# Clustered attention followed by a SwiGLU layer on one core: how q and k of groups 3 to 7 are loaded and transposed

## The chip, the cores and the metric

The kernel runs on one core of a Trainium2 chip. The metric is device time in microseconds (us), the median of several runs. A profile of one execution is used beside it; its times are counted from the start of its span.

## The reference, cut to what matters

Attention in which a query only sees the keys of its own cluster, then a gated feed-forward layer over all heads:

```python
B, H, S, D = 4, 8, 768, 64            # 16 centroids for each head
q_assign = argmax(q_n @ c_n.T); k_assign = argmax(k_n @ c_n.T)    # nearest centroid
mask = q_assign[..., :, None] == k_assign[..., None, :]
scores = where(mask, q @ k.T / sqrt(D), -1e9)
attn = softmax(scores) @ v
x = attn.transpose(0, 2, 1, 3).reshape(B * S, H * D)              # 3072 x 512
xn = x / rms(x) * rms_g
out = (silu(xn @ w_gate) * (xn @ w_val)) @ w_out                  # 512 -> 1536 -> 512
```

All inputs and the output are float32 in HBM.

## The kernel before, in words

**Groups and units.** The 32 (batch, head) pairs are numbered n = 0 to 31 and taken in eight groups of four heads (g = 0 to 7, so a batch is two groups). The attention and the feed-forward work run in eight units of half a batch: unit u covers 384 queries of batch u // 2 for all eight heads. A unit has 24 gaps (8 heads, three each); at each gap `scores` (line 323) issues two score matmuls, L333, and one exponential on ScalarE, L337. `pv` (line 341) multiplies the probabilities with v, L351, and VectorE divides and stores, L356 and L358.

**The mask.** For each head a tile `qext` or `kext` holds the transposed q or k in 64 rows and a one-hot of its cluster in 16 further rows, so that one matmul of depth 80 gives the scores and the mask. Both have four buffers, one for each of four groups.

**From HBM to `qext` and `kext`.** `load` (line 80) brings q or k of one head to a staging tile `qk` with 128 partitions, in each six tokens of 64 numbers, 1536 bytes without a break. The tile holds q and k; there are six (`NQ`), so the load of head n + 6 waits until head n has been used. `trans` (line 202) transposes with three TensorE matmuls against an identity (L208) into a PSUM tile `tq`; ScalarE (L214), or VectorE for some heads of the second batch (L212), copies it to `qkT` and scales k by 1/2048 on the way. `cast` (line 220, instruction L227) makes bf16 halves of 64 partitions of it, on GpSimd for q, on VectorE for k in group 3 and later. `cluster_steps` (line 255) multiplies with the centroids (L241), transposes (L244), finds the largest and makes the one-hot (L249, L253), transposes back (L271), and `place` (line 277) sends it with 16 small DMAs (L282) to the last rows of `qext` and `kext`: 8 for q and 8 for k. For group 2 these 16 DMAs are issued by SyncE's queue (SP), for groups 3 to 7 by GpSimd's (POOL). Groups 0 and 1 are placed by VectorE (`under`, L317).

**What sets the order.** The order on each engine is written out. Unit 0 uses a table of work for each gap, `first`. In the other units `attention` (line 636) walks through the gaps and fills in work from a list, each piece with a cost; pieces are issued so that the summed cost keeps pace with the gaps. `group_work` (line 468), which makes the pieces of one group, gives each `trans` 0.3 and the rest of the preparation mostly 0. Unit 1 does the casts of group 2 and the transposes of group 3; unit u from 2 to 5 prepares group u + 2. The feed-forward work of earlier units makes up the rest: `gv` (gate and val, L423, with the tanh L431 and the products L432 and L436 on VectorE) and `out_mm` (L448). Gate, val, tq, sc, tx and o take turns in the three PSUM buffers of the tag `gen`.

**The SP queue.** It issues, in order, the loads of q, k and v, the 16 DMAs of `place` of group 2, and the stores of the output. In the stretch that matters it issues: q and k of heads 12 and 13, v of heads 8 to 15, q and k of head 14, v 16, q and k of 15, v 17, q and k of 16, v 18, q and k of 17, v 19, then `place` of group 2 (four DMAs for the first half of q, eight for k, four for the second half of q), then q, k and v of later heads. The load of v 16 waits until GpSimd has read v 8 (L230). The DMAs of the SP and ACT queues share eight semaphores in turn, and each DMA waits for the landing of the one eight before it. The weights are loaded by GpSimd's queue (L194, L197), with a cast to bf16, four pairs of w_gate and w_val and three pieces of w_out.

**Squares.** `squares` (L373 on VectorE, L376 on ScalarE) sums the squares of a unit's rows; VectorE does it for units 0 and 1, ScalarE for the rest.

Of the kernel before, what the change touches and what calls it, by code (L numbers as in the profile page):

```python
# [18 lines left out]
ZS = 2048.0  # L19
# [3 lines left out]
def kernel(  # L23
# [12 lines left out]
    nc = tc.nc  # L36
    B, H, S, D = q.shape
# [5 lines left out]
    HT = ST // 2  # L43
    UQ = HT * P
    HG = 4
# [8 lines left out]
    CUT = CC + 2 * FC - 8  # L54
    LEAD = 6
    NQ, NV = 6, 8

    ctx.enter_context(tc.manual_schedule())
    pool = lambda n, b, **kw: ctx.enter_context(tc.tile_pool(name=n, bufs=b, **kw))
# [14 lines left out]
    staged, stagedv = {}, {}  # L74

    def src(a, n):
        b, h = divmod(n, H)
        return a[b, h].rearrange("(p t) d -> p t d", t=ST)

    def load(n, part, on=None):  # L80
        if n not in staged:
            staged[n] = stage.tile([P, 2, ST, D], F32, tag="qk", name="qk")
        (on or nc.sync).dma_start(out=staged[n][:, part], in_=src((q, k)[part], n))

    def load_qk(n):
        if n < B * H:
            load(n, 0)
            load(n, 1)

    def load_v(n, vq=None):  # L90
        if n >= B * H:
            return
        stagedv[n] = stage.tile([P, ST, D], F32, tag="vs", name="vs", bufs=NV)
        (vq or nc.sync).dma_start(out=stagedv[n], in_=src(v, n))

    c_in = const.tile([P, D], F32)
    nc.sync.dma_start(out=c_in, in_=centroids.rearrange("h c d -> (h c) d"))
    load(0, 0)
    load(0, 1, nc.scalar)
    load(1, 1, nc.scalar)  # L100
# [49 lines left out]
    for i in range(P // 32):  # L150
        r = slice(32 * i, 32 * i + 32)
# [48 lines left out]
    qkT = {}  # L200

    def trans(g, h, part, on=None):
        if (g, h // 2) not in qkT:
            qkT[g, h // 2] = qk32.tile([P, 2, 2, UQ], F32, tag="qkT", name="qkT")
        qk = staged[g * HG + h]
        ps = ps_g.tile([P, UQ], F32, tag="gen", name="tq")
        for i in range(HT):
            nc.tensor.transpose(ps[:, i * P:(i + 1) * P], qk[:, part, 2 * i:2 * i + 2].rearrange("p t d -> p (t d)"),  # L208
                                ident_f)
        to, by = qkT[g, h // 2][:, h % 2, part], 1.0 / ZS if part else 1.0  # L210
        if on is nc.vector:
            nc.vector.tensor_scalar_mul(to, ps, by)  # L212
        else:
            nc.scalar.activation(to, ps, ACT.Copy, scale=by)  # L214

    def cols(of, g, e, a=0, b=UQ):

        return of.rearrange("p (x e) -> p x e", e=2)[:, a:b, e] if g < H // HG else of[:, e * UQ + a:e * UQ + b]

    def cast(on, g, h, part, es=(0, 1)):  # L220
        for e in es:
            to = cols((kext if part else qext)[g % 4][:D, h], g, e)
            of = qkT[g, h // 2][e * D:(e + 1) * D, h % 2, part]
            if on is nc.scalar:
                nc.scalar.copy(to, of)
            else:
                on.tensor_copy(to, of)  # L227

    def vcast(n):
        nc.gpsimd.tensor_copy(vbf[n // HG % 4][:, n % HG, :, :D], stagedv[n])  # L230
# [24 lines left out]
    def cluster_steps(g, m):  # L255

        of = {}

        def products():
            of["cl"] = cluster_products(g, [(h, m) for h in range(HG)])  # L260

        def most():
            of["mx"] = largest(of["cl"])

        def same():
            of["ohT"] = asg.tile([P, UQ], BF16, tag="ohT", name="ohT", bufs=2)
            compare(of["ohT"].rearrange("p (b e c) -> p b e c", e=2, c=NC), of["cl"], of["mx"])

        def back():
            put[g, m] = asg.tile([P, UQ], BF16, tag="oh", name="oh", bufs=3)  # L270
            nc.vector.transpose(put[g, m], of["ohT"])  # L271

        return [products, most, same, back]
# [3 lines left out]
    def place(on, g, m, es=(0, 1)):  # L277

        ext = (kext if m else qext)[g % 4]
        for h in range(HG):  # L280
            for e in es:
                on.dma_start(out=ext[D:D + NC, h, e * UQ:(e + 1) * UQ],  # L282
                             in_=put[g, m][32 * h + e * NC:32 * h + (e + 1) * NC])
# [82 lines left out]
    def squares(u, t, last):  # L366
        if (t, last) == (0, False):
            sq[u] = small.tile([P, 2, HT], F32, tag="ss", name="ss")
            xn[u] = xp.tile([P, HT, DM], BF16, tag="xn", name="xn")
        c = slice(DM - 2 * D, DM) if last else slice(0, DM - 2 * D)  # L370
        to = sq[u][:, int(last), t:t + 1]
        if u <= 1:
            nc.vector.scalar_tensor_tensor(xn[u][:, t, c], xs[u][:, t, c], 1.0 / DM, xs[u][:, t, c], op0=ALU.mult,  # L373
                                           op1=ALU.mult, accum_out=to)
        else:
            nc.scalar.activation(xn[u][:, t, c], xs[u][:, t, c], ACT.Square, scale=DM ** -0.5, accum_out=to)  # L376

    def rms(u):
        x, nt = xs[u], UNITS[u][2]
        for t in range(nt):  # L380
            squares(u, t, True)
        ms = small.tile([P, HT], F32, tag="ms", name="ms")
        nc.vector.scalar_tensor_tensor(ms[:, :nt], sq[u][:, 0, :nt], 1e-6, sq[u][:, 1, :nt], op0=ALU.add, op1=ALU.add)
        y = rsqrt(ms[:, :nt], nt)
        for t in range(nt):
            nc.vector.tensor_scalar_mul(xn[u][:, t], x[:, t], y[:, t:t + 1])
# [81 lines left out]
    def group_work(g):  # L468

        t, c = [], []  # L470
        for h in range(HG):
            n = g * HG + h
            t += [(0.3, lambda h=h: trans(g, h, 0)), (0.3, lambda h=h: trans(g, h, 1))]

            def others(n=n):
                vcast(n)
                load_qk(n + NQ)
                load_v(n + NV)

            def both(h=h, f=others):  # L480
                cast(nc.gpsimd, g, h, 0)
                f()
                cast(nc.vector, g, h, 1, (0,))
            if g == 2:
                c.append((0.0, others))
            else:
                c += [(0.0, both), (0.0, lambda h=h: cast(nc.vector, g, h, 1, (1,)))]
        a = []
        for m in range(2):
            a += [(0.0 if i else 0.7, f) for i, f in enumerate(cluster_steps(g, m))]  # L490
            if g == 3:
                a.append((0.0, lambda m=m: place(nc.gpsimd, g, m)))
            elif g == 2:
                a.append((0.0, (lambda: (place(nc.sync, g, 1), place(nc.sync, g, 0, (1,)))) if m else
                          (lambda: place(nc.sync, g, 0, (0,)))))
        if g > 3:
            a[:1] = [(1.4, lambda f=(a[0][1], a.pop(4)[1]): [x() for x in f])]
            a.append((0.0, lambda: [place(nc.gpsimd, g, m) for m in range(2)]))
        return t, c, a
# [5 lines left out]
    def group(g):  # L505
        t, c, a = group_work(g)
        return [x for h in range(HG) for x in t[2 * h:2 * h + 2] + c[2 * h:2 * h + 2]] + a
# [13 lines left out]
    def ffn_work(u):  # L521
        n = UNITS[u][2] / HT
        w = [(0.18 * n, lambda c=c: xtrans(u, c)) for c in range(CC)]
        for f in range(FC):
            for val in (False, True):
                w.append((0.64 * n, lambda f=f, val=val: gv(u, f, val)))
        return w

    def out_work(u):
        return [(0.86, lambda t=t, p=p: out_mm(u, t, p)) for t in range(UNITS[u][2]) for p in range(3)]  # L530
# [6 lines left out]
    def tokens(g, h, on=None):  # L537
        trans(g, h, 1, on)
        trans(g, h, 0, on)
# [96 lines left out]
    def attention(heads, fill, skip=0, hooks={}):  # L636
        gaps = [(u, h, i) for u, h in heads for i in range(UNITS[u][2])]
        total, done, n = sum(c for c, _ in fill), 0.0, 0
        for at, (u, h, i) in enumerate(gaps):
            scores(u, h, i)  # L640
            if i == (0 if (u, h) == (1, 0) else 1):
                for p in due:
                    pv(*p)
                due[:] = [(u, h)]
            if h == H - 1:
                squares(u, i, False)
            if (u, h, i) in hooks:
                hooks[u, h, i]()
            while n < len(fill) and at >= skip and done <= total * (at + 1 - skip) / (len(gaps) - skip):
                done += fill[n][0]  # L650
                fill[n][1]()
                n += 1
        for _, f in fill[n:]:
            f()

    attention([(0, h) for h in range(H)], [], hooks={(0, *divmod(i, HT)): f for i in range(H * HT) for f in [first.get(i, more)] if f})
    for u in range(1, NU):
        ffn, o, g = ffn_work(u - 1), out_work(u - 2) if u > 1 else [], u + 2
        if u == 1:
            t, c, a = group_work(2)  # L660
            t3, c3, a3 = group_work(3)
            n = LEAD - 4
# [60 lines left out]
```

The softmax here doesn't subtract the row's maximum and nothing guards it: scores larger than these inputs give would overflow.

## Time and profile before

| what | value |
|---|---|
| median of 3 runs | 345.44 us (345.31 to 345.99) |
| span of the profiled execution | 343.6 us |
| its own time | not recorded apart from the runs; they are 1.7 to 2.4 us above the span |
| TensorE busy | 336.0 us, 98% of the span |
| VectorE busy | 219.9 us, 64% |
| ScalarE busy | 259.7 us, 76% |
| GpSimd busy | 112.9 us, 33% |
| granted TensorE clock | 1.000 |
| transposes L208 | 192, of 276 ns each |
| first score matmul of units 1 to 5 | 33.1, 64.8, 106.6, 147.6, 188.7 us |

A row of the costliest groups reads: line, engine, operation, output<-inputs, shapes, count, then the busy time and the mean length of one, then the idle time of the engine just before them and what ended it. The timeline has start, length, engine, line and operation; neighbours of a kind are merged, and "x4" says how many. Matmuls overlap: the length of one says less than the distance from one start to the next. The answer on DMA gives, for a stretch, the packets and the share of the 16 DMA engines of each queue: q1 is the SP queue, q0 is GpSimd's. Below it are the DMAs issued in the stretch, with the median time from issue to landing.

### The profile page before, as it was taken

Reading aid. Unit: us, or ns where it says so; the run is one execution under the profiler, and the core shown is the slowest. Engines: PE = TensorE matmul, PEld = TensorE weight load, DVE = VectorE, ACT = ScalarE, POOL = GpSimd, SP = SyncE. Lnnn points to the kernel's source line nnn. Section 1 sums busy time; section 2 is a strip of 40 time slices with the busy share of each in tenths; the row PEclk is TensorE's granted clock in tenths of the full one; section 3 lists DMA queues with packets and bytes.
Section 4 is the critical chain, followed back from the end, with each engine's and each line's share of the span. In section 5 each row is a group of like instructions: output and inputs, shape, how many; then the busy total and the mean of one; then the engine's idle time right before and its main releaser. Section 6 shows DMA issues by size and latency. Waiting matters only on the chain.

```text
span 343.6 us, 8003 instructions
## 1 busy us (share of the span) xinstructions
PE 336.0 (98%) x3045; PEld 208.2 (61%) x3045; DVE 219.9 (64%) x540; ACT 259.7 (76%) x449; POOL 112.9 (33%) x225
## 2 busy tenths in 40 slices
PE   8999999999999999999999999999999999999996
PEld 3547657555766567665675656756566656655654
DVE  6999796975577626785367745686455635575330
ACT  5899979856979768786797777888688877763322
POOL 6999596234335305271131801516000000000000
PEclk9999999999999999999999999999999999999999
DMA  8999989882450015401130011000100011001002
GB/s 276 384 210 216 248 166 237 134 267 97 149 158 14 31 62 152 139 18 40 61 94 2 23 53 41 2 5 21 63 32 0 2 46 49 2 1 64 31 2 92
DMA packets 27302, 31.62 MB, mean 92 GB/s; under 512 B 4480, under 2 KB 24320, under 8 KB 27264
## 3 DMA queue, kind: packets, MB, share of 16 engines
q1 hardware_dynamic: 18608, 25.02, 22.2%
q0 software_dynamic: 8368, 5.71, 10.4%
q8 instruction: 24, 0.39, 0.5%
q10 hardware_dynamic: 288, 0.39, 0.4%
q14 instruction: 14, 0.11, 0.1%
HBM read 28.35 MB, written 6.29 MB: 101 GB/s over the span
## 4 chain that ended last, share of the span: by engine, by line
PE 82%; ACT 9%; DVE 6%; DMA 1%; issue 1%; DVEq 0%; ACTq 0%
PE o L448 17%; PE val L423 16%; PE gate L423 16%; PE s L333 15%; PE acc L351 9%; ACT pT L337 6%; PE tq L208 4%; PE sc L241 3%; PE tx L396 1%; ACT xn L376 1%; ACT th L431 1%; DVE pads L312 1%; DVE kext L317 1%; DVE qext L317 1%; DMA c_in<-in_centroids_dram 1%
## 5 line engine op out<-in xcount | busy, mean ns | idle before, releaser
L337 ACT ACTIVATE pT<-s,off 128x768 bf16<-128x768 f32 x192 | 171.3, 905 | 39.7 <-PE s L333 38.7
L333 PE MATMUL s<-qext,kext 80*128 80x384 bf16 x384 | 94.8, 327 | 2.4 <-ACT pT L337 1.6
L432 DVE SCALAR_TENSOR_TENSOR th<-th,gate 128x384 f32<-128x384 f32 x84 | 46.4, 552 | 50.8 <-ACT th L431 50.6
L423 PE MATMUL gate<-xnT,wg 128*128 128x384 bf16 x384 | 78.5, 325 | 0.1
L423 PE MATMUL val<-xnT,wv 128*128 128x384 bf16 x384 | 78.1, 326 | 0.1
L448 PE MATMUL o<-wo,gvT 128*128 128x512 bf16 x276 | 67.6, 379 | 0.0
L227 POOL CAST qext<-qkT 64x384 bf16<-64x384 f32 x64 | 35.3, 558 | 72.3 <-ACT qkT L214 63.8
L333 PEld LDWEIGHTS <-kext 80*128 80x128 bf16 x384 | 36.4, 98 | 35.1 <-issue 9.9
L436 DVE SCALAR_TENSOR_TENSOR gvT<-th,val 128x384 bf16<-128x384 f32 x84 | 46.3, 551 | 6.8 <-PE val L423 2.0
L423 PEld LDWEIGHTS <-wv 128*128 128x128 bf16 x384 | 36.3, 97 | 22.4 <-issue 0.7
L423 PEld LDWEIGHTS <-wg 128*128 128x128 bf16 x384 | 36.2, 97 | 22.0 <-issue 0.8
L351 PEld LDWEIGHTS <-pT 128*128 128x128 bf16 x1152 | 43.4, 97 | 10.1 <-DVE x L358 1.0
L431 ACT ACTIVATE th<-gate 128x384 f32<-128x384 f32 x84 | 41.3, 492 | 9.4 <-PE gate L423 8.8
L351 PE MATMUL acc<-vbf,pT 128*128 128x65 bf16 x1152 | 45.7, 193 | 0.6 <-ACT pT L337 0.2
L448 PEld LDWEIGHTS <-gvT 128*128 128x128 bf16 x276 | 25.6, 97 | 25.2 <-issue 0.6
L208 PE MATMUL tq<-ident_f,qk 128*128 128x128 f32 x192 | 30.9, 276 | 0.0
L282 POOL DMA_DIRECT2D qext<-oh x40 | 19.1, 486 | 34.7 <-DVE oh L271 28.3
L214 ACT ACTIVATE qkT<-tq 128x384 f32<-128x384 f32 x57 | 27.4, 494 | 3.4 <-PE tq L208 2.9
L397 DVE TENSOR_SCALAR xnT<-tx,gcol 128x384 bf16<-128x384 bf16 x28 | 10.4, 412 | 27.5 <-PE tx L396 27.5
L208 PEld LDWEIGHTS tq<-ident_f,qk 128*128 128x128 f32 x192 | 23.2, 141 | 6.6 <-ACT qkT L214 1.0
L451 ACT COPY o_sb<-o 128x512 f32<-128x512 f32 x23 | 13.5, 586 | 15.5 <-PE o L448 15.5
L282 POOL DMA_DIRECT2D kext<-oh x40 | 19.1, 485 | 9.6 <-DVE oh L271 9.6
(81 smaller groups left out, 246.2 us busy)
## 6 DMA issues: line engine op xcount, KB each, us to landing
qk<-in_q_dram SPq DMA_DIRECT2D x32, 192.0 KB, 3.9
vs<-in_v_dram SPq DMA_DIRECT2D x32, 192.0 KB, 4.2
out_dram<-o_sb SPq DMA_DIRECT2D x23, 256.0 KB, 2.0
qk<-in_k_dram SPq DMA_DIRECT2D x30, 192.0 KB, 3.9
wg<-in_moe_w_gate_dram POOLq DMA_DIRECT2D x4, 384.0 KB, 8.7
wv<-in_moe_w_val_dram POOLq DMA_DIRECT2D x4, 384.0 KB, 11.0
wo<-in_moe_w_out_dram POOLq DMA_DIRECT2D x3, 512.0 KB, 8.9
qext<-oh POOLq DMA_DIRECT2D x40, 12.0 KB, 1.6
```

What stands on the lines that cost most here:

```text
L208: nc.tensor.transpose(ps[:, i * P:(i + 1) * P], qk[:, part, 2 * i:2 * i + 2].rearrange("p t d -> p (t d)"), ident_f)
L214: nc.scalar.activation(to, ps, ACT.Copy, scale=by)
L227: on.tensor_copy(to, of)
L282: on.dma_start(out=ext[D:D + NC, h, e * UQ:(e + 1) * UQ], in_=put[g, m][32 * h + e * NC:32 * h + (e + 1) * NC])
L333: nc.tensor.matmul(ps[:, j, :w] if nt == HT else flat[:, j * w:(j + 1) * w], lhsT=cols(kext[g % 4][:KR, hh], g, kc // HT, kc % HT * P, (kc ...
L337: nc.scalar.activation(pT[u, h][:, n * i:n * i + n, :w], of, ACT.Exp, bias=off, scale=scale * ZS)
L351: nc.tensor.matmul(acc[:, h % 2, t], lhsT=pT[u, h][:, kc, t * P:(t + 1) * P], rhs=vbf[g % 4][:, hh, kc % HT * 2 + kc // HT], start=kc == 0 ...
L423: nc.tensor.matmul(ps, lhsT=w[:, c, f * P:(f + 1) * P], rhs=xnT[u][:, c, :n], start=c == 0, stop=c == CC - 1)
L431: nc.scalar.activation(th, ps, ACT.Tanh, scale=0.5)
L432: nc.vector.scalar_tensor_tensor(th, th, 1.0, ps, op0=ALU.add, op1=ALU.mult)
L436: nc.vector.scalar_tensor_tensor(gvT[u][:, f, :n], gates[u], 0.5, ps, op0=ALU.mult, op1=ALU.mult)
L448: nc.tensor.matmul(outs[u], lhsT=gvT[u][:, f, t * P:(t + 1) * P], rhs=wo[:, f], start=f == 0, stop=f == FC - 1)
```

## The change

For the 20 heads of groups 3 to 7 (`BG = 3`):

- Each load of q or k, one DMA with 128 rows of 1536 bytes, becomes four DMAs on the SP queue. Each fills 32 partitions with 12 pieces of 128 bytes, half of a token's row, so that the tokens lie where a transpose of 32x32 blocks puts them in the right place.
- `trans` becomes one VectorE instruction that transposes the 32x32 blocks of a 128x384 tile from the staging tile to `qkT`. The three matmuls L208, the PSUM tile `tq` and the copy L214 are gone for these heads.
- The factor 1/2048 of k moves from that copy to the cast, which for k becomes a multiplication.
- The cost of these transposes in the list is 0.0 instead of 0.3.
- The squares of unit 1 move from VectorE to ScalarE.

```diff
+    BG = 3
...
     def load(n, part, on=None):
         if n not in staged:
             staged[n] = stage.tile([P, 2, ST, D], F32, tag="qk", name="qk")
-        (on or nc.sync).dma_start(out=staged[n][:, part], in_=src((q, k)[part], n))
+        if n < BG * HG:
+            (on or nc.sync).dma_start(out=staged[n][:, part], in_=src((q, k)[part], n))
+            return
+
+        to = staged[n][:, part].rearrange("p t d -> p (t d)").rearrange("p (i r d) -> p i r d", i=HT, d=32)
+        of = (q, k)[part][n // H, n % H].rearrange("(r p i e) (c d) -> e c p i r d", p=32, i=HT, e=2, d=32)
+        for e in range(2):
+            for c in range(2):
+                r = 32 * (2 * e + c)
+                nc.sync.dma_start(out=to[r:r + 32], in_=of[e, c])
...
         qk = staged[g * HG + h]
+        if g >= BG:
+            nc.vector.transpose(qkT[g, h // 2][:, h % 2, part], qk[:, part].rearrange("p t d -> p (t d)"))
+            return
         ps = ps_g.tile([P, UQ], F32, tag="gen", name="tq")
...
-            if on is nc.scalar:
+            if part and g >= BG:
+                on.tensor_scalar_mul(to, of, 1.0 / ZS)
+            elif on is nc.scalar:
...
-        if u <= 1:
+        if u == 0:
             nc.vector.scalar_tensor_tensor(xn[u][:, t, c], xs[u][:, t, c], 1.0 / DM, xs[u][:, t, c], op0=ALU.mult,
                                            op1=ALU.mult, accum_out=to)
...
-            t += [(0.3, lambda h=h: trans(g, h, 0)), (0.3, lambda h=h: trans(g, h, 1))]
+            w = 0.0 if g >= BG else 0.3
+            t += [(w, lambda h=h: trans(g, h, 0)), (w, lambda h=h: trans(g, h, 1))]
```

## The prediction

> **What bounds the kernel now.** I read the page first: busy times, then the chain that ended last.
>
> ```profile
> PE 336.0 (98%) x3045; PEld 208.2 (61%) x3045; DVE 219.9 (64%) x540; ACT 259.7 (76%) x449; POOL 112.9 (33%) x225
> ...
> PE 82%; ACT 9%; DVE 6%; DMA 1%; issue 1%; DVEq 0%; ACTq 0%
> ```
>
> TensorE has no idle time worth the name, and the chain is 82% TensorE, 4% of it the transposes L208. To price those I read TensorE's timeline in unit 4, where group 6 is prepared:
>
> ```profile
> 172.61 0.49 PE L208 MATMUL tq<-ident_f,qk 128*128 128x128 f32 x3
> 172.94 0.49 PE L333 MATMUL s<-qext,kext 80*128 80x384 bf16 x2
> 173.27 0.49 PE L208 MATMUL tq<-ident_f,qk 128*128 128x128 f32 x3
> ```
>
> Three transposes hold TensorE from 172.61 to 172.94, 0.33 us, though each lasts 276 ns.
>
> Then the place where the changed loads could matter: the SP queue ahead of unit 2, and the scores that need what it sends.
>
> ```profile
> 48.72 0.39 SPq L83 DMA_DIRECT2D qk<-in_q_dram  x1
> 49.15 0.42 SPq L83 DMA_DIRECT2D qk<-in_k_dram  x1
> ...
> 52.90 0.37 SPq L94 DMA_DIRECT2D vs<-in_v_dram  x1
> 53.48 3.24 SPq L282 DMA_DIRECT2D qext<-oh  x4
> 56.82 7.75 SPq L282 DMA_DIRECT2D kext<-oh  x8
> ```
>
> ```profile
> L282 SPq DMA_DIRECT2D kext<-oh x2: 507/507/507, 59.2 to 60.0; - x2
> ...
> DMA to landing us min/median/max: 5.2/5.6/5.9
> ```
>
> ```profile
> 64.81 0.98 PE L333 MATMUL s<-qext,kext 80*128 80x384 bf16 x4
> ```
>
> The one-hot of group 2 goes out behind six loads. The second DMA for k (59.2, the answer for `kext` in 58 to 60) lands 5.9 us later, at 65.1. The "x4" is the first two gaps of unit 2; a pair takes 0.49 us elsewhere, so the second one starts 0.49 us before the end, at 65.3, and needs just that half of k. So the slack is 0.2 us, without a wait: a later `place` stops TensorE.
>
> The last view is the DMA answer for 20.5 to 23.5, where a load of 512 elements of 4 bytes (the gains, 9.2 us to landing) ran beside the weights:
>
> ```profile
> DMA packets 1179, 0.53 MB, mean 176 GB/s; under 512 B 533, under 2 KB 1179, under 8 KB 1179
> ...
> q0 software_dynamic: 628, 0.47, 104.3%
> q1 hardware_dynamic: 551, 0.06, 28.8%
> ```
>
> In 3 us, 551 packets of the SP queue went beside 628 of the weights, about one for one, though the SP queue's were tiny: 184 per us.
>
> **What the Trainium skill says.** "DMA: Bandwidth & Descriptors", section Queues, rings and completion order: each DMA engine goes round between queues packet by packet. The view above agrees (551 to 628). The same page, Specifications: line rate wants 512 bytes or more for a transfer. No run shows 128-byte pieces yet. "TensorE: Matmul & The Clock Gate", Part 4: a 128x128 transpose takes about 275 ns in a kernel. The rows say 276, but in a stream the price is 0.33 / 3 = 0.11 us.
>
> **Removed.** 20 heads x 2 = 40 transposes of three matmuls: 40 x 0.33 = 13.2 us of TensorE, 2.64 us in each of the units 1 to 5. 40 copies L214 at 494 ns leave ScalarE, which isn't the bound; worth nothing by itself. The PSUM tile `tq` is gone too, which eases the three `gen` buffers.
>
> **Added on VectorE.** 40 block transposes. The nearest row, L317, is from SBUF, 384 columns of 4 bytes, 572 ns; two of L244 take 1.05 us together, so 0.5 us each in a stream; 40 x 0.5 = 20 us. Bounds: 0.35 us (as the casts L227) to 0.6. The cast with a factor stays at 355 ns: L386, a multiplication of 512 columns, takes 483, so one of 384 about the same as the cast; nothing either way. In 168.8 to 184.2 (windows), the stretch of unit 4 with the transposes, VectorE is busy 10.39 of 15.40 us. Eight transposes make it 10.39 + 8 x 0.5 = 14.4, while TensorE has 15.40 - 2.64 = 12.8 left. VectorE frees gate and val, so it becomes the limit there: the gain is 15.4 - 14.4 = 1.0 us, not 2.64. Units 2 to 5: 4 x 1.0 = 4.0 us. Bounds: 0, if the later mask steps of VectorE pile up as well, and 4 x 2.64 = 10.6, if the three buffers and its idle time behind this stretch absorb the excess. GpSimd's casts of q now wait for VectorE; GpSimd is idle there (19 waits, 64.6 us).
>
> **Moved: squares of unit 1.** Three squares of 527 ns and three of 298 with six read-outs of 198, 3.7 us, go from VectorE to ScalarE, around the start of unit 2. TensorE waits for `place` there by the next step, so nothing; without that cover up to 2.2 us (three times 527 + 198 ns).
>
> **Added on the SP queue.** Before `place` of group 2 it issues 12 loads of heads 12 to 17. They become 48 DMAs of 32 x 12 = 384 packets, 18,432 instead of 1,536. The 12 loads of v stay, 1,536 packets. From 27.1 us on:
> - Weights still to come: 2,382 packets in 27 to 48 and 1,455 in 48 to 66 (q0, DMA answers), 3,837. Each lets one packet of SP's through: 3,837 / 184 = 20.9 us for 3,837 of its 19,968.
> - The other 16,131 go alone. A tiny packet held an engine for 28.8% x 16 x 3 us / 551 = 25 ns, so 16 engines take 640 per us: 25.2 us. The v packets are longer, 1,536 at 246 per us (2,224 less 250 small ones in the 8 us of 7 to 15) are 6.2 us instead of 2.4: 3.8 more.
> - Sum 49.9: the loads end at 27.1 + 49.9 = 77.0 us. `place` follows in the queue; its sixth DMA lands some 1.6 us later (median of the quiet ones), at 78.6.
>
> The second gap of unit 2 moves from 65.1 to 78.6, by 13.5 us. Nothing covers it: TensorE's list is in order, and what stands behind these scores waits. The 2.64 us saved in unit 1 only lengthen the wait; the wait of the SP queue for GpSimd (11.2 us at 48.3) is used up, that is in the sum. Heads 14 and 15 come late for VectorE too (now used at 53.6 to 59.0); this runs inside the same delay.
>
> Bounds of the rate, which no trace shows for 128 bytes: 960 per us, if an issue each 0.40 us is the limit (384 / 0.4), gives 20.9 + 16.8 + 3.8 = 41.5, `place` landing at 70.2 and a delay of 5.1 us; 400 per us gives 20.9 + 40.3 + 3.8 = 65.0, so 93.7 and 28.6 us. Below nothing it can't go, since the packets are twelve times as many. I take 640, the row of the trace with the smallest packets.
>
> **Added later on.** 32 more DMAs per unit instead of 8: 12,288 packets at 640 are 19 us of a unit of 41, for heads used 40 us later: nothing. Below 300 per us it would not fit. The stores of the output wait behind loads; three buffers are needed again only a unit later: nothing. `place` of the later groups has a unit of time.
>
> **Sum.** 343.6 + 13.5 - 4.0 = 353.1 us of span. The runs lie 1.7 to 2.4 us above the span, the median 1.84. So 345.44 + 9.5 = 354.9, say 355.
>
> **Rivals.**
> - *Slow descriptors* (400 per us or less): a queue of small pieces is bound by something other than the engines. For it: the 4-byte load took 9.2 us to land. Against: weights ran beside it. 345.44 + 28.6 - 4.0 = 370.
> - *Fast descriptors* (960): delay 5.1, and 345.44 + 5.1 - 4.0 = 346.5, or up to 350 with rates between.
> - *Faster in the end.* One mechanism: VectorE's excess is absorbed by the `gen` buffers that `tq` no longer takes, so units 2 to 5 give 10.6 us, against the 5.1 of the fast queue: 345.44 - 5.5 = 339.9. It decides once the gain of a unit exceeds a quarter of the delay, 1.3 us at the fast rate, 3.4 (more than there is) at mine. For it: VectorE is busy only 64% overall. Against: 14.4 against 12.8 us where it counts.
> - *The change does nothing*: excluded, since the listing of TensorE's instructions has 40 transposes of three fewer.
>
> **How the numbers follow.** Forecast (349 to 362 us) 0.50; slow descriptors (above 362) 0.21; fast ones (346.2 to 349) 0.13; faster 0.12; the rest, 0.04, within 0.2%, about what a measurement of this kernel can tell from no change. Slower is 0.50 + 0.21 + 0.13 = 0.84. The range runs from 343 to 372: below it some 0.09 of the faster case, above it 0.08.
>
> **What would show it.** Right: TensorE idle in front of L333 at the start of unit 2, ended by the DMA of `kext`, at 70 us or later; small packets and weights about one for one; in units 2 to 5 a VectorE nearly full in the stretch of the transposes, and each unit shorter by about 1 us. Wrong: no wait there, or units shorter by over 2 us; a wait of VectorE for `qk` in every unit would mean the queue can't keep up at all.

## The result, and the profile after

The kernel with the change takes 360.72 us (median of 4 runs, 359.83 to 361.81), the one before 345.47 us beside it: a ratio of 1.0438, 95% interval 1.0412 to 1.0463. It is 15.3 us slower; the forecast was 9.5 us slower. The profiled span is 360.0 us against 343.6; the profiled run is the slowest of the four, 361.81 us.

The page: busy times, the granted clock in 40 slices of 9 us, and the chain that ended last.

```profile
PE 330.3 (92%) x2925; PEld 195.5 (54%) x2925; DVE 238.0 (66%) x568; ACT 246.6 (69%) x421; POOL 112.6 (31%) x225
...
PEclk9999999557999999999999999999999999999999
...
PE 62%; DVE 13%; DMA 8%; ACT 6%; SPq 6%; issue 4%; DVEq 0%; POOL 0%; ACTq 0%; POOLq 0%
```

TensorE has less work, but it is no longer full: 92% instead of 98%. On the chain VectorE has 13% instead of 6% and the DMAs 8% instead of 1%, the SP queue is new with 6%, and in three slices the clock is down. The first score matmuls of the units (TensorE's timeline; line 333 is now L348) say where:

| | before, us | after, us | difference |
|---|---|---|---|
| start of unit 1 | 33.09 | 33.73 | +0.6 |
| unit 1 | 31.72 | 46.02 | +14.3 |
| unit 2 | 41.79 | 44.00 | +2.2 |
| units 3 to 5 together | 123.09 | 122.38 | -0.7 |
| unit 6 to the end | 113.9 | 113.9 | 0 |

All of the loss is made by 124 us, most of it at the end of unit 1. The waits, from the list of all engines (total, times, longest):

```profile
PE s L348 <- DMA kext<-oh: 9.8, 1, 9.8
...
PE sc L256 <- DVE th L447: 8.2, 5, 3.9
...
DVE qkT L217 <- DMA qk<-in_k_dram: 4.0, 2, 3.7
```

One wait of 9.8 us for the one-hot that `place` sends, as foreseen, and one of 3.9 us that names VectorE. VectorE itself stood 3.7 us for a k still on its way. TensorE's timeline has the two stops in order:

```profile
66.42 1.51 PE L256 MATMUL sc<-qkT,cblk 128*32 128x384 f32 x8 [3.93 <-DVE th L447]
67.86 0.82 PE L348 MATMUL s<-qext,kext 80*128 80x384 bf16 x2
68.47 1.48 PE L438 MATMUL val<-xnT,wv 128*128 128x384 bf16 x4
79.75 1.44 PE L348 MATMUL s<-qext,kext 80*128 80x384 bf16 x4 [9.79 <-DMA kext<-oh]
```

The wait is put down to `th`, but that product (L447) stands behind a block transpose (L217) in VectorE's order, and the transpose waited for k:

```profile
65.35 0.58 DVE L217 STREAM_TRANSPOSE qkT<-qk 128x384 f32<-128x384 f32 x1 [3.65 <-DMA qk<-in_k_dram]
65.85 0.52 DVE L447 SCALAR_TENSOR_TENSOR th<-th,gate 128x384 f32<-128x384 f32 x1
```

So the late one is the load of head 15. Then unit 2 waits for `place`. On the SP queue (start, length):

```profile
69.33 2.58 SPq L93 DMA_DIRECT2D qk<-in_q_dram  x4
71.95 2.65 SPq L93 DMA_DIRECT2D qk<-in_k_dram  x4
74.70 0.56 SPq L104 DMA_DIRECT2D vs<-in_v_dram  x1
75.35 2.47 SPq L297 DMA_DIRECT2D qext<-oh  x4
77.92 5.54 SPq L297 DMA_DIRECT2D kext<-oh  x8
```

`place` is issued from 75.35 instead of 53.48, 21.9 us later. From the rows between 27 and 75 us: the twelve loads hold the queue 37.2 us instead of 6.3, those of v 9.0 instead of 7.0, and the 11.2 us in which it used to wait for GpSimd are gone: 30.9 + 2.0 - 11.2 = 21.7. A load with no weights beside it holds the queue some 2.6 us (the first two rows above); twelve of them would be 31.2, so 6.0 of the 37.2 us came on top, most of it while the weights were on their way.

Windows (stretch, length, busy time of PE, PEld, DVE, ACT, POOL, granted clock, DMA share, GB/s):

```profile
70.00:80.00 10.00, 0.25 (x1) 0.14 (x2) 1.59 (x3) 0.12 (x2) 3.86 (x8) 0.50 0.45 94
80.00:84.00 4.00, 4.00 (x29) 2.42 (x28) 0.75 (x2) 2.18 (x3) 0.00 (x0) 0.50 0.08 20
84.00:88.00 4.00, 4.00 (x23) 2.22 (x22) 2.22 (x4) 2.17 (x4) 0.00 (x0) 0.84 0.14 28
88.00:92.00 4.00, 4.00 (x42) 2.36 (x44) 2.21 (x4) 3.41 (x11) 0.00 (x0) 1.00 0.46 72
```

When TensorE resumes at 79.75 it is at half clock, and 0.84 in the third row puts the return at 85.3 (1.28 us at half, the rest full): 5.5 us of work at half speed, 2.8 us lost. The Trainium skill, "TensorE: Matmul & The Clock Gate", Part 1, has both steps, half rate after an idle window of about 3.4 us and full rate after about as long a busy one. Here the clock was at 0.50 from 66 us on (windows of 2 us), after the first stop of 3.93 us, and the return took 5.5 us of work, longer than the page's figure. The forecast had no such term.

Last, the stretch of unit 4 with the mask work of group 6:

```profile
187.33:201.30 13.97, 12.17 (x109) 6.62 (x107) 13.56 (x31) 8.26 (x13) 6.07 (x12) 1.00 0.37 61
```

VectorE is busy 13.56 of 13.97 us and TensorE idle for 1.8.

### The profile page after: what moved, and what is told of

The parts are those of the page before. It is cut to its first block, busy times and chain, and to the rows that moved or that the text cites. A ratio compares the mean times of both kernels' runs of the same rounds, so it can differ in the third digit from the quotient of the medians.

```text
span 360.0 us, 7928 instructions
## 1 busy us (share of the span) xinstructions
PE 330.3 (92%) x2925; PEld 195.5 (54%) x2925; DVE 238.0 (66%) x568; ACT 246.6 (69%) x421; POOL 112.6 (31%) x225
## 4 chain that ended last, share of the span: by engine, by line
PE 62%; DVE 13%; DMA 8%; ACT 6%; SPq 6%; issue 4%; DVEq 0%; POOL 0%; ACTq 0%; POOLq 0%
PE o L463 17%; PE s L348 12%; PE gate L438 11%; PE val L438 11%; PE acc L366 7%; SPq L93 5%; ACT pT L352 3%; DMA qk<-in_q_dram 3%; DVE qkT L217 2%; DMA qk<-in_k_dram 2%; DVE th L447 2%; DVE kext L238 2%; PE sc L256 2%; PE tx L411 1%; ACT xn L391 1%
## 5 line engine op out<-in xcount | busy, mean ns | idle before, releaser
L348 PE MATMUL s<-qext,kext 80*128 80x384 bf16 x384 | 95.9, 331 | 12.7 <-DMA kext<-oh 9.8
L438 PE MATMUL val<-xnT,wv 128*128 128x384 bf16 x384 | 79.4, 329 | 3.3 <-DVE th L447 2.7
L447 DVE SCALAR_TENSOR_TENSOR th<-th,gate 128x384 f32<-128x384 f32 x84 | 45.9, 546 | 29.1 <-ACT th L446 28.7
L348 PEld LDWEIGHTS <-kext 80*128 80x128 bf16 x384 | 36.4, 99 | 48.5 <-issue 21.9
L412 DVE TENSOR_SCALAR xnT<-tx,gcol 128x384 bf16<-128x384 bf16 x28 | 10.4, 413 | 30.9 <-PE tx L411 30.9
L217 DVE STREAM_TRANSPOSE qkT<-qk 128x384 f32<-128x384 f32 x40 | 22.2, 565 | 4.2 <-DMA qk<-in_k_dram 4.0
L466 ACT COPY o_sb<-o 128x512 f32<-128x512 f32 x23 | 13.5, 586 | 14.0 <-PE o L463 14.0
L373 DVE TENSOR_TENSOR x<-acc,inv 128x384 f32<-128x384 f32 x32 | 17.8, 557 | 1.1
L256 PE MATMUL sc<-qkT,cblk 128*32 128x384 f32 x96 | 10.9, 527 | 8.2 <-DVE th L447 8.2
```

What stands on the lines that cost most here:

```text
L217: nc.vector.transpose(qkT[g, h // 2][:, h % 2, part], qk[:, part].rearrange("p t d -> p (t d)"))
L256: nc.tensor.matmul(ps[32 * i:32 * i + 32], lhsT=cblk[:, g * HG % H + h], rhs=qkT[g, h // 2][:, h % 2, m], start=True, stop=True)
L348: nc.tensor.matmul(ps[:, j, :w] if nt == HT else flat[:, j * w:(j + 1) * w], lhsT=cols(kext[g % 4][:KR, hh], g, kc // HT, kc % HT * P, (kc ...
L438: nc.tensor.matmul(ps, lhsT=w[:, c, f * P:(f + 1) * P], rhs=xnT[u][:, c, :n], start=c == 0, stop=c == CC - 1)
L447: nc.vector.scalar_tensor_tensor(th, th, 1.0, ps, op0=ALU.add, op1=ALU.mult)
```

## The experiments

The theory of the forecast (Q in the expectations below): the loads hold the SP queue, `place` stands behind them, and that is the loss; the saving on TensorE is mostly lost to a full VectorE. Rival one (V below): VectorE with its new transposes is late at the end of unit 1 and makes the loss (the 3.9 us wait names it). Rival two, on the loads: the DMA engines choke on 128-byte pieces, and the queue is only the place where it shows. The kernel before took 345.78 to 345.98 us beside these runs (medians).

**Loads without transposes.** The kernel before with the new form of the loads alone; TensorE still transposes.

```diff
...
+        to = staged[n][:, part].rearrange("p t d -> p (t d)").rearrange("p (i r d) -> p i r d", i=HT, d=32)
+        of = (q, k)[part][n // H, n % H].rearrange("(r p i e) (c d) -> e c p i r d", p=32, i=HT, e=2, d=32)
+        for e in range(2):
+            for c in range(2):
+                r = 32 * (2 * e + c)
+                nc.sync.dma_start(out=to[r:r + 32], in_=of[e, c])
```

> The kernel before, but q and k of groups 3 to 7 are loaded as in the changed kernel, in four DMAs of 128-byte pieces; TensorE still transposes (the tokens stand in another order inside a head, so the output is another one). Theory Q, the SP queue: the cost is the time that 48 small DMAs hold the queue, so nearly all of it is here too: unit 2 starts at 78 to 81 us instead of 64.8, time 359 to 363. Rival V, VectorE: the cost comes from VectorE, which stands still for a late head and has 20 us more to do; then this kernel loses only what TensorE waits for late heads, unit 2 starts before 72 and the time is below 354.

Measured: 362.4 us, ratio 1.047 (1.0439 to 1.05). TensorE's timeline has the same two stops:

```profile
66.98 0.52 PE L218 MATMUL tq<-ident_f,qk 128*128 128x128 f32 x3 [3.39 <-DMA qk<-in_k_dram]
...
80.30 1.44 PE L343 MATMUL s<-qext,kext 80*128 80x384 bf16 x4 [5.75 <-DMA kext<-oh]
```

Without a single new instruction on VectorE the loss is all there, within the range expected. Rival one falls.

**Transposes without the loads.** The changed kernel with each load one DMA of 1536-byte rows again.

```diff
-        if n < BG * HG:
+        if True:
```

> The changed kernel with its loads left as before, one DMA of 1536-byte rows (the blocks then hold other tokens, so the output is another one). Theory Q: no wait at the start of unit 2; unit 2 starts at about 65 as before, since the one-hot of group 2 lands no earlier; units 3 to 5 are shorter by 0.1 to 0.3 us each, as in the changed kernel: 344.5 to 345.5 us. The forecast's 1.0 us a unit would give 341.5; TensorE's saving in full (2.64 us a unit) 335. Rival V: 350 or more.

Measured: 345.2 us, ratio 0.9985 (0.9966 to 1.0004). Units 3 to 5 take 40.9, 40.7 and 40.7 us, as in the changed kernel. 13.2 us less work for TensorE buys nothing that the median can tell from zero. One thing was not expected: unit 1 gets 1.4 us shorter, but unit 2 takes 44.77 us instead of 41.79, for TensorE now reaches `place` before it has landed:

```profile
66.07 0.42 PE L348 MATMUL s<-qext,kext 80*128 80x384 bf16 x1 [1.55 <-DMA kext<-oh]
```

That trace is of a run of 346.51 us, and the twenty lie between 343.84 and 348.72, so how often this stop comes is not known. A full VectorE is therefore shown as the limit only for units 3 to 5, which gave 0.8 us together; at the start of unit 2 `place` took back what unit 1 had gained.

**`place` of group 2 on GpSimd's queue**, with the small loads kept.

```diff
-                a.append((0.0, (lambda: (place(nc.sync, g, 1), place(nc.sync, g, 0, (1,)))) if m else
-                          (lambda: place(nc.sync, g, 0, (0,)))))
+                a.append((0.0, (lambda: (place(nc.gpsimd, g, 1), place(nc.gpsimd, g, 0, (1,)))) if m else
+                          (lambda: place(nc.gpsimd, g, 0, (0,)))))
```

> The changed kernel, with the 16 DMAs of the one-hot of group 2 issued by GpSimd's queue, not behind the loads of heads 15 to 17 on SP's. Theory Q: the 9.8 us wait for the one-hot goes; what is left is the 4 us for k of head 15, so unit 2 starts at 68 to 71 and, with less of TensorE's halved clock, the time is 347 to 350. Rival: another late load takes the place of this wait, and the time stays above 356.

Measured: 345.67 us, ratio 0.999 (0.9979 to 1.0002). Unit 2 starts at 65.34, and the clock is 1.00 throughout. 15 us come back from moving 16 DMAs to another queue, so the loss was made by their place in the SP queue. The expectation, 347 to 350 us, was too slow: it left 2 to 4 us for the late k of head 15, but that wait shrank from 3.7 to 0.7 us. These loads are issued only 0.7 us sooner than in the changed kernel (57.01 instead of 57.73 for the k of head 15), so most of it lies after the issue. The edit moved something else as well: the w_out loads now stand behind `place` in GpSimd's queue, and the first is issued at 60.50 instead of 51.83. The share of GpSimd's queue in the 16 DMA engines while k of head 15 was on its way, first in the changed kernel (60 to 65 us), then here (57 to 62 us):

```profile
q0 software_dynamic: 530, 0.53, 74.0%
```

```profile
q0 software_dynamic: 204, 0.08, 5.8%
```

That fits the shorter wait; no run moves the weights alone.

**Fewer groups in the new form.** `BG = 5`: groups 3 and 4, the ones loaded while the weights still come, stay as before.

```diff
-    BG = 3
+    BG = 5
```

> The changed kernel with the half-row loads and block transposes from group 5 on only (BG = 5), so that no small piece stands ahead of the one-hot of group 2. Theory Q: no wait at unit 2; units 3 to 5 give 0.1 to 0.3 us each: 344.5 to 345.5 us. Rival V, VectorE's load or half-row loads cost in every unit: each of three units longer, 347 or more.

Measured: 344.87 us, ratio 0.998 (0.9959 to 1.0002). Unit 2 starts at 64.99. The loss goes with those loads, and no `place` or weight load has changed its queue here; units 3 to 5 are shorter by 0.15, 0.29 and 0.36 us.

**What in the loads costs it: DMAs or pieces.** Three kernels from the one before, with nothing else of the change. Four DMAs of 32 whole rows, 1536 bytes each:

```diff
...
+        for r in range(0, P, 32):
+            nc.sync.dma_start(out=staged[n][r:r + 32, part], in_=src((q, k)[part], n)[r:r + 32])
```

> The kernel before; each load of q and k of groups 3 to 7 is four DMAs of 32 whole rows (1536 bytes, 32 pieces) instead of one of 128 rows. Two theories of what makes a small DMA hold the SP queue for 0.65 us in the changed kernel. By the piece: the number of 128-byte pieces does it (384 of them); then the 32 pieces here take 0.35 us or so an issue, 1.5 us a load, unit 2 starts near 70 and the time is 349 to 352. By the DMA: each takes 0.65 us whatever is in it, so unit 2 starts at 78 to 81 and the time is 360 to 363.

Two DMAs of 128 partitions, six pieces of 128 bytes in each:

```diff
...
+        to = staged[n][:, part].rearrange("p t d -> p (t d)")
+        of = (q, k)[part][n // H, n % H].rearrange("(p t) (c d) -> c p t d", t=ST, d=32)
+        for c in range(2):
+            nc.sync.dma_start(out=to[:, c * UQ // 2:(c + 1) * UQ // 2].rearrange("p (t d) -> p t d", d=32), in_=of[c])
```

> The kernel before; each of those loads is two DMAs of 128 partitions x 6 pieces of 128 bytes, 768 pieces each (the halves of the tokens then stand apart in the tile, so the output is another one). By the piece: 1.3 us an issue, 2.6 us a load as in the changed kernel, and 360 to 363 us. By the DMA: 0.65 us an issue, 1.3 us a load, and 348 to 352 us.

One DMA of 128 partitions, twelve pieces of 128 bytes in each:

```diff
...
+        to = staged[n][:, part].rearrange("p t d -> p (t d)").rearrange("p (t d) -> p t d", d=32)
+        b, h = divmod(n, H)
+        of = (q, k)[part][b].rearrange("h s d -> (h s) d")[h // 2 * 2 * S:(h // 2 * 2 + 2) * S]
+        nc.sync.dma_start(out=to, in_=of.rearrange("(p t) (c d) -> c p t d", t=2 * ST, d=32)[h % 2])
```

> The kernel before, with every load of q and k of groups 3 to 7 as one DMA of 128 partitions of 12 pieces of 128 bytes, 1536 pieces; a head's tile gets half rows of its own and its neighbour's tokens, so other numbers, of the same size, are transposed. In the kernels so far a DMA with 128-byte pieces held the SP queue 0.65 us, with 384 pieces as with 768. If that is a price of the DMA, the twelve loads hold it 12 x 0.65 = 7.8 us instead of 4.8, unit 2 starts 3 us late or so, and the median is 347 to 350 us. If a DMA of 1536 pieces holds it for 1.3 us or more, the time is that of two_dmas_halves, 355.5 to 358. If the DMA engines are the limit[...], it lies at 352 to 357, with the SP queue's instructions long[...].

Measured. The last two columns are the median length of a DMA of q on the SP queue, from the view of its line, and the summed length of the twelve loads that stand ahead of `place`, from the queue's instructions:

| a load is | median, us (95% of the ratio) | unit 2 starts, us | a DMA of q holds SP, us | twelve loads, us |
|---|---|---|---|---|
| before: 1 DMA, 128 rows of 1536 B | 345.8 to 346.0 | 64.81 | 0.36 | 6.3 |
| 4 DMAs, 32 rows of 1536 B | 354.68 (1.0226 to 1.0271) | 71.12 | 0.41 | 21.3 |
| 1 DMA, 1536 pieces of 128 B | 354.61 (1.0241 to 1.0305) | 70.16 | 0.54 | 16.2 |
| 2 DMAs, 768 pieces | 356.68 (1.0273 to 1.0351) | 75.28 | 0.64 | 29.8 |
| 4 DMAs, 384 pieces (loads without transposes) | 362.4 (1.0439 to 1.05) | 80.30 | 0.62 | 35.0 |

Both count. The second row has the old number of pieces and still brings unit 2 6.3 us late: there it is the number of DMAs alone. Besides the 21.3 us of issue, that queue stood still for some 9 us in 13 waits that each ended within 0.1 us of the landing of the DMA eight before, as the order of the eight semaphores asks. The third has the old number of DMAs, and unit 2 is 5.4 us late: there it is the pieces. What a DMA of q holds of the queue does not grow with its pieces: 0.54 us for 1536, 0.62 for 384. The k right behind a q of 1536 pieces held it longer, 1.09 us in the median. The kernels with four DMAs of rows and with two DMAs both came between their two expectations, so neither price alone gives the time; the third expectation for the single DMA, the engines as the limit, came true (352 to 357 us). The change's four DMAs cost the queue 4 x 0.65 = 2.6 us a load, 384 / 0.65 = 590 pieces per us, while the 16 DMA engines are little more than half busy (DMA share 0.61 and 0.52 in the two stretches from 70 to 74 us of the changed kernel). In the single-DMA kernel this price was not the limit. Its rows are short and long by turns, while the windows show the engines without a pause (DMA share 1.12 from 54 to 60, 1.27 from 60 to 66):

```profile
59.07 0.55 SPq L89 DMA_DIRECT2D qk<-in_q_dram  x1
59.68 1.55 SPq L89 DMA_DIRECT2D qk<-in_k_dram  x1
61.33 2.94 SPq L100 DMA_DIRECT2D vs<-in_v_dram  x1
```

So rival two holds a part. Of the 15.5 us by which the change's loads delay unit 2, the pieces alone make 5.4 and the four DMAs alone 6.3; the other 3.8 come only when both meet, so how the whole is shared out between the two is not settled.

What a piece takes of an engine: the changed kernel's DMA answers for 40 to 43 us, beside the weights, and for 90 to 104, without them, and last the single-DMA kernel's for 80 to 84, also without them (packets, MB, share of the 16 engines):

```profile
q0 software_dynamic: 718, 0.54, 114.1%
q1 hardware_dynamic: 711, 0.09, 37.8%
```

```profile
q1 hardware_dynamic: 7412, 1.27, 50.7%
```

```profile
q1 hardware_dynamic: 4077, 0.70, 98.3%
```

Beside weights 0.378 x 16 x 3 / 711 = 25.5 ns; alone at most 0.507 x 16 x 14 / 7412 = 15.3 ns, since 256 longer packets of v are among them. In the last answer the engines are full and take 4,077 packets in 4 us, 1,019 per us.

**The squares of unit 1.** The kernel with `place` on GpSimd's queue, where no wait covers them, with the squares back on VectorE.

```diff
-        if u == 0:
+        if u <= 1:
```

> The kernel with place of group 2 on GpSimd's queue, with the squares of unit 1 back on VectorE, as before the change. The forecast gave this part of the change nothing as long as the wait for place covers it, and up to 2.2 us without that cover; in this kernel the cover is gone. If the squares matter, the median is 346.5 to 348 us instead of 345.7, with unit 2 longer or later. If VectorE has room there, it stays within 0.3 us.

Measured: 347.52 us, ratio to before 1.0041 (1.0018 to 1.0065), where that kernel with the squares on ScalarE had 0.999 (0.9979 to 1.0002). Unit 2 takes 43.99 us instead of 42.32. TensorE's wait behind VectorE there is longer:

```profile
71.57 0.81 PE L438 MATMUL val<-xnT,wv 128*128 128x384 bf16 x4 [1.40 <-DVE th L447]
```

It was shorter with the squares on ScalarE:

```profile
69.80 0.81 PE L438 MATMUL val<-xnT,wv 128*128 128x384 bf16 x4 [0.81 <-DVE th L447]
```

So the squares' move gains 1.8 us once `place` is on time, and without it the transposes on VectorE would be a small loss even with `place` on time.

**VectorE relieved.** The kernel with `place` on GpSimd's queue, with the casts of k for groups 4 to 7 on GpSimd.

```diff
-                cast(nc.vector, g, h, 1, (0,))
+                cast(nc.gpsimd if g > 3 else nc.vector, g, h, 1, (0,))
...
-                c += [(0.0, both), (0.0, lambda h=h: cast(nc.vector, g, h, 1, (1,)))]
+                c += [(0.0, both), (0.0, lambda h=h: cast(nc.gpsimd if g > 3 else nc.vector, g, h, 1, (1,)))]
```

> place_pool, with the casts of k from group 4 on given from VectorE to GpSimd. If VectorE is what holds units 2 to 5 (13.56 of 13.97 us busy in the stretch of the transposes), 8 x 0.36 = 2.9 us less for it in each make the units 1.7 to 2.3 us shorter (TensorE stood still 1.8 us there): 337 to 339.5 us. If something else holds them (TensorE's own order, ScalarE), the time stays at 345 to 346.

Measured: 336.34 us, ratio 0.9726 (0.97 to 0.9751). That is a little below the range expected. Units 3 to 5 take 38.5 us each, 2.5 less than before: nearly all of the 2.64 us that the transposes cost TensorE. TensorE's waits from 100 to 230 us, first with the casts on VectorE, then with them on GpSimd:

```profile
PE sc L256 <- DVE th L447: 4.2, 4, 1.0
PE val L438 <- DVE th L447: 2.0, 5, 0.6
PE s L348 <- ACT pT L352: 0.8, 3, 0.3
```

```profile
PE s L348 <- ACT pT L352: 0.8, 3, 0.3
```

Both waits for VectorE are gone. It was the limit, not the transposes' data or GpSimd. The kernel before with nothing but its casts moved was not run; its TensorE is idle for only 0.26 of the 41.03 us of unit 4, so little can come from the casts alone.

**The same with `BG = 4`**, so that group 3 is loaded and transposed as before.

> The same with BG = 4, so that heads 12 to 15 are loaded and transposed as before. By the SP queue, head 15's k is no longer late, and the start of unit 2 is as before, 64 to 65 us; group 3's transposes are back on TensorE in unit 1 (2 us). Within 1 us of pool_casts: 336 to 339.5 us. If VectorE doesn't hold the units: 345 to 346.

Measured: 335.98 us, ratio 0.9713 (0.9698 to 0.9727), the lowest median here, though the runs do not tell it from the one with `BG = 3`. Its page, busy times and chain:

```profile
PE 326.7 (98%) x2949; PEld 197.0 (59%) x2949; DVE 222.1 (66%) x528; ACT 248.9 (74%) x429; POOL 159.0 (48%) x273
...
PE 81%; ACT 10%; DVE 6%; issue 1%; DMA 1%; DVEq 0%; ACTq 0%
```

TensorE is the bound again, with 9.3 us less to do than before.

## Why the prediction was right in kind and too small

- **`place` behind the loads: right.** The wait that was named came, at the line named, ended by the DMA of `kext`; moving `place` off the queue took the loss away. Forecast 13.5 us later; unit 1 grew by 14.3, and the scores that need `place` could start at 79.75, where the forecast had 78.6. That the two lie so close is in part luck. The loads were out at 75.35 instead of 77.0, but `place` took 4.4 us from there instead of 1.6: the forecast counted only its landing and not the four DMAs of q that go ahead of k.
- **The rate: right size, wrong reason, so luck.** 640 pieces per us came from 25 ns of engine time. The shares behind it add up to more than the engines have (104.3% + 28.8%), so the packets overlap in that count, and 25 ns is not what one costs. With the engines full and no weights beside them they took 1,019 per us. What held the queue near 590 was the issue, 0.65 us for each DMA of small pieces, where the fast bound had assumed 0.40 as for whole rows. That bound (346.5 us) failed by this price.
- **One for one with the weights: right only while the weights fill the engines; the term was too large.** 711 packets went beside 718 from 40 to 43 us, but 1,372 beside 348 from 38 to 40, and 20,538 beside 4,077 from 27.8 to 75.4. The forecast's 20.9 us for 3,837 packets are 14.9 more than they would take at 640 per us; the loads held the queue only 6.0 us beyond 12 x 2.6. The sum came near, 47.6 us (27.77 to 75.35) for 49.9, since other terms were too small: v 9.0 for 6.2, the loads alone 31.2 for 28.8.
- **Heads 14 and 15 late "inside the same delay": right in the sum.** They made a stop of their own, 3.9 us, but `place` came later still.
- **Units 2 to 5 shorter by 1.0 us each: the term most off among those written down.** Units 3 to 5 gave 0.14, 0.29 and 0.28 us. In unit 4 VectorE has 29.99 us to do instead of 26.07, which is eight transposes at 0.49, so the price was right. The stretch was cut too short: it ended at 184.2, ahead of the mask steps and products that follow and fill VectorE too (before, 3.51 of the 4 us from 181 to 185). The forecast's own lower bound, 0, "if the later mask steps of VectorE pile up as well", is what came. TensorE has 2.1 us less to do in that unit and is idle 1.8 us more.
- **The clock: a term that was missing.** 2.8 us in unit 2, for work at half rate after the long stop. Unit 2 grew by 2.2 instead of shrinking by 1.0.
- **Squares: a gain of 1.8 us without the cover of the wait.** The forecast named up to 2.2 and no direction; it reckoned with ScalarE's lengths (527, 298 and 198 ns are those of L376). That the move is worth nothing under the cover was not run.
- **The sum.** Forecast 13.5 - 4.0 = 9.5. Measured on the span 0.6 + 14.3 + 2.2 - 0.7 = 16.4. Of the 6.9 us between, 3.2 lie in unit 2 (2.2 for -1.0), 2.3 in units 3 to 5, 0.8 in unit 1 and 0.6 ahead of it. The last is a spread that other kernels show too, with the start of unit 1 between 33.0 and 34.1.

The rivals: slow descriptors (370 us, 400 per us or less) fell, for the queue ran near 590 per us where the weights were not in its way (3,072 pieces from 69.33 to 74.60 us). Faster in the end needed VectorE's excess absorbed by the buffers; units 3 to 5 with the old loads and the experiment with the casts moved show that it was not.

## What to carry to other kernels

Before a load is cut into more DMAs, count what stands behind it on the same queue and how much slack that has: here, with 0.2 us of slack, 16 tiny DMAs behind the cut loads cost 15 us, and another queue gave it back. Work taken off the bounding engine is worth what the next engine leaves of it in that stretch, so carry the stretch on to the point where that engine has caught up; here eight transposes at 0.49 us ate a saving of 2.64 us until eight casts of 0.36 us were taken off VectorE. To the price of a wait of TensorE belongs the half-speed work that can follow it, here 2.8 us.

## What the runs showed of the hardware that was not expected

- A DMA on the SP queue holds it for 0.36 to 0.41 us with 1536-byte rows (128 or 32 of them) and for 0.54 to 0.64 us with 128-byte pieces (medians of the loads of q), no longer for 1536 pieces than for 384. What makes the difference is open.
- The half clock needs no long stop: in the changed kernel with plain loads TensorE stood for 1.55 us up to 66.07, and its clock was at a mean of 0.54 and 0.61 in the next two stretches of 2 us; windows of 0.5 us put the half clock from about 66.2 to 69.6. A wait of 1.40 us, in the kernel with the squares back on VectorE, left the clock at 1.00.
- GpSimd takes 1.17 us for the cast of k with a factor, 64 x 384, and 0.5 us for the one of q without:

```profile
L238 POOL TENSOR_SCALAR kext<-qkT x32: 1160/1166/1170, 91.5 to 220.7; 64x384 bf16<-64x384 f32 x32
```

  VectorE does it in about 0.36. It was still the better place, because GpSimd had the time.
